# Seven-product first-layer groups: three of four in the last two blocks, with the second layer's first product moved in between

## The chip, the cores and the metric

One core of a Trainium2 chip runs the whole kernel. The metric is the device time of one execution in microseconds (us). The kernel before took 297.75 us (median of three runs, 297.69 to 301.05). Its profiled execution took 297.95 us, of which 296.1 us are the span from the first to the last instruction in the trace.

## The reference

Eight batches, eight heads, 576 positions of head size 64 go through a retention layer (attention without softmax, with a decay per head). Its output, 4608 tokens of 512 channels, goes through a two-layer network with a tanh GELU:

```python
scores = scale * np.matmul(q, k.transpose(0, 1, 3, 2))
ret = scores * Dmat[None, :, :, :]           # Dmat[h, i, j] = gamma_h ** (i - j) for i >= j, else 0
x = np.matmul(ret, v)                        # turned into 4608 x 512
h = x @ w_in                                 # 512 -> 2048
g = 0.5 * h * (1.0 + np.tanh(c * (h + 0.044715 * h * h * h)))
out = g @ w_out                              # 2048 -> 512
```

The change concerns the last two lines alone.

## The kernel before, in words

The kernel is written with the order of every engine's instructions fixed by hand: each engine executes its instructions in the order in which the Python code issues them, and semaphores make it wait where it reads or overwrites what another engine has not finished. TensorE (PE) multiplies into PSUM, of which there are eight banks of 128 x 512 float32 numbers; `bank` takes the bank that has been free longest, `drop` gives one back. ScalarE (ACT) and VectorE (DVE) read PSUM.

The 4608 tokens are taken in nine blocks of 512, `t` = 0 to 8. Blocks 0 to 7 are the first 512 positions of the eight batches; block 8 is made of the last 64 positions of all eight. The retention layer of batch t+1 is worked between the matmuls of block t (the `events`, run at a given step of a block). Blocks 7 and 8 have no retention layer beside them except that of the last tails in block 7.

A block has two layers. Its first layer makes 16 chunks of 128 of the 2048 hidden columns. A plain chunk (`up`) is four matmuls of 512 tokens into one bank `hp` (L471), and one GELU by ACT into the tile `gT` (L477). The second layer is always done by the Strassen-Winograd scheme: tokens and hidden columns are cut in halves, and seven products of half size take the place of eight (`prod`). Each product m has a part for u = 0 and one for u = 1, of eight matmuls of 256 columns each (L661). They land in banks `opA` (products 1 and 2), `opB` (6, 7), `opC` (5, 3) and, in the last two blocks, `opD` (4). The sums of activations that the products need (`act_sums`: s1, s2, an in-place difference in `gT`, s4) are made by DVE, and `after` adds the products up into the two output tiles `o0` and `o1` and stores them.

In the last two blocks (`WIN`) the first layer uses the seven-product scheme too, for two of its four groups. A group j is four chunks: two among the lower eight (`lo`) and two among the upper eight (`hi`). `up_prod(t, j, m)` is product m of group j: four matmuls of 256 columns (L560). Product 1 opens bank `hB`, and ACT copies it to a work tile `s` (L580). Product 2 goes to `hA`, DVE adds it to `s` (L567), and ACT makes the GELU of the sum (L570). Product 6 adds to `hB`, which ACT copies to `v` (L586); product 7 adds to `hB` again, which DVE copies to `u3` and sums with product 5 in `hC` (L588, L589), with a GELU after that; product 4 adds to `hB` and is read by a GELU directly; product 3 adds to `hC`, and `v` plus `hC` gets the last GELU. So one group costs ACT two copies and four GELUs, and DVE one copy and three additions. The sums of weights (`in_sums`) and of the layer's input (`x_sums`) are made by DVE in the second layer of block 6, and of block 7 for block 8's input.

`W_ORDER` is the order of a block's first layer: "mj" is product m of group j, an empty token is the next plain chunk, "aN" is `act_sums` for chunks 2N and 2N+1. After it come the products of the second layer in the order 1, 4, 6, 5, 7, 2, 3.

At the end of block 8, `end` stores each half of an output tile as two stores of 64 rows, one issued by SyncE's queue (SP) and one by ACT's: twelve stores in all. The last product, 3, is read out in two halves: DVE adds the half of u = 0 (L713 in the code calls `add`, whose line is L675) before the half of u = 1 is multiplied into the same bank `opC`.

Of the kernel before, what the change touches and what calls it, by code (L numbers as in the profile page):

```python
# [20 lines left out]
def kernel(  # L21
# [476 lines left out]
        )  # L498
        drop(hp)

    WIN = {t: 2 for t in (NTB - 2, NTB - 1)}
    GW = max(WIN.values())
    wi = {}

    def in_sums(j, ns):
        if not wi:
            for n in "234":
                wi[n] = sb.tile([128, 2, 256 * GW], F16, tag="ld", name="wi" + n, bufs=LD)
        c, lo, hi = slice(256 * j, 256 * j + 256), slice(256 * j, 256 * j + 256), slice(DF // 2 + 256 * j, DF // 2 + 256 * j + 256)
        b11, b12, b21, b22 = w_in_sb[:, 0:2, lo], w_in_sb[:, 0:2, hi], w_in_sb[:, 2:4, lo], w_in_sb[:, 2:4, hi]  # L510
        t2, t3, t4 = (wi[n][:, :, c] for n in "234")
        for n in ns:
            o, x, y, f = {
                3: (t3, b22, b12, ALU.subtract), 2: (t2, t3, b11, ALU.add),
                4: (t4, b21, t2, ALU.subtract), 1: (b12, b12, b11, ALU.subtract),
            }[n]
            nc.vector.tensor_tensor(out=o, in0=x, in1=y, op=f)
# [3 lines left out]
    def x_sums(t):  # L521
        if not xw:
            for n in ("12", "34"):
                x = sb.tile([128, 2, 4, 2, TL], F16, tag="ld", name="x" + n, bufs=LD)
                xw[int(n[0])], xw[int(n[1])] = x[:, 0], x[:, 1]
            for n in range(2):
                for s in "svu":
                    wk[s, n] = sb.tile([128, 512], F32, tag="ld", name="w" + s, bufs=LD)
        o = 8 * (t % 2) if t < B else GM
        x = xT[:, o : o + 8]  # L530
        a11, a12, a21, a22 = x[:, 0:4, 0:2], x[:, 0:4, 2:4], x[:, 4:8, 0:2], x[:, 4:8, 2:4]
        for s, x, y, f in (
            (xw[1], a21, a22, ALU.add), (xw[2], xw[1], a11, ALU.subtract),
            (xw[3], a11, a21, ALU.subtract), (xw[4], a12, xw[2], ALU.subtract),
        ):
            nc.vector.tensor_tensor(out=s, in0=x, in1=y, op=f)

    wk, wb = {}, {}

    def up_prod(t, j, m):  # L540
        if t not in gT:
            gT[t] = sb.tile([128, NF, NI, 128], F16, tag="gT", name="gT", bufs=1)
        o = 8 * (t % 2) if t < B else GM
        lo, hi = 256 * j, DF // 2 + 256 * j
        xh = lambda u, k: lambda kt: xT[:, o + 4 * u : o + 4 * u + 4, 2 * k + kt, :]
        xs = lambda n: lambda kt: xw[n][:, :, kt, :]
        ws = lambda k, c: lambda kt, i: w_in_sb[:, 2 * k + kt, c + 128 * i : c + 128 * i + 128]
        wt_ = lambda n: lambda kt, i: wi[n][:, kt, lo + 128 * i : lo + 128 * i + 128]
        tag, x, w = {
            1: ("B", xh(0, 0), ws(0, lo)), 2: ("A", xh(0, 1), ws(1, lo)), 3: ("C", xs(4), ws(1, hi)),  # L550
            4: ("B", xh(1, 1), wt_("4")), 5: ("C", xs(1), ws(0, hi)), 6: ("B", xs(2), wt_("2")),
# [6 lines left out]
        for i in range(2):  # L558
            for kt in range(2):
# [1 line left out]
                    pb[:, 256 * i : 256 * i + 256].rearrange("p (g t) -> p g t", t=TL), w(kt, i), x(kt),  # L561
                    start=(new and i == kt == 0), stop=(kt == 1), skip_group_check=True,
                )
        s, v, u3 = (wk[n, j % 2] for n in "svu")

        def add(o, a, b):
            nc.vector.tensor_tensor(out=o, in0=a, in1=b, op=ALU.add)  # L567

        def gelu(x, u, f):
            nc.scalar.activation(  # L570
                out=gT[t][:, f : f + 2, 2 * u : 2 * u + 2, :].rearrange("p f i n -> p f (i n)"),
                in_=x.rearrange("p (f n) -> p f n", f=2), func=AF.Gelu_apprx_tanh,
            )

        def free(tag):
            drop(wb.pop((j, tag)))
# [2 lines left out]
        if m == 1:  # L579
            nc.scalar.copy(out=s, in_=pb)  # L580
        elif m == 2:
            add(s, s, pb)
            free("A")
            gelu(s, 0, f)
        elif m == 6:
            nc.scalar.copy(out=v, in_=pb)  # L586
        elif m == 7:
            nc.vector.tensor_copy(out=u3, in_=pb)  # L588
            add(u3, u3, wb[j, "C"])  # L589
            gelu(u3, 1, NH + f)  # L590
        elif m == 4:
            gelu(pb, 1, f)
            free("B")
        elif m == 3:
            add(v, v, pb)
            free("C")
            gelu(v, 0, NH + f)
# [35 lines left out]

    gs = {}

    def act_sums(t, f0, f1, us=slice(0, 2)):
        if t not in gs:
            gs[t] = {n: sb.tile([128, NH, 2, 128], F16, tag="s" + n, name="s" + n, bufs=1) for n in ("1", "2", "4")}
        g = gT[t].rearrange("p f (u i) n -> p f u i n", i=2)
        lo, hi = slice(f0, f1), slice(NH + f0, NH + f1)  # L640
        a11, a12, a21, a22 = g[:, lo, us, 0], g[:, hi, us, 0], g[:, lo, us, 1], g[:, hi, us, 1]
        s = {n: x[:, lo, us] for n, x in gs[t].items()}
        nc.vector.tensor_tensor(out=s["1"], in0=a21, in1=a22, op=ALU.add)  # L643
        nc.vector.tensor_tensor(out=s["2"], in0=s["1"], in1=a11, op=ALU.subtract)
        nc.vector.tensor_tensor(out=a21, in0=a11, in1=a21, op=ALU.subtract)
        nc.vector.tensor_tensor(out=s["4"], in0=a12, in1=s["2"], op=ALU.subtract)  # L646

    def prod(t, m, u):
        g = gT[t].rearrange("p f (u i) n -> p f u i n", i=2)
# [4 lines left out]
        }[m]  # L654
        rhs = {1: W11, 2: W21, 3: W22, 4: wt["4"], 5: wt["1"], 6: wt["2"], 7: wt["3"]}[m]
        tag = {1: "A", 2: "A", 3: "C", 4: "D" if t in WIN else "B", 5: "C", 6: "B", 7: "B"}[m]
        new = m in (1, 6, 5) or tag == "D"
        if new and u == 0:
            op[tag] = bank("op" + tag)
        for f in range(NH):  # L660
            nc.tensor.matmul(  # L661
                op[tag][:, HD * u : HD * u + HD], lhs(f), rhs[:, f],
                start=(new and u == 0 and f == 0), stop=(f == NH - 1), skip_group_check=True,
            )

    keep = {}

    def after(t, m, u):
        last = t == NTB - 1
        if u == 0 and not (last and m == 3) or m == 4 and t in WIN:  # L670
            return
        def pr(tag):
            return op[tag].rearrange("p (u d) -> p u d", u=2)
# [9 lines left out]
                end(o[:, v], i, v)  # L683
        def end(o, i, v, d=slice(0, DM)):
            b = 4 * v + 2 * i
            for h, e in enumerate((nc.sync, nc.scalar)):
                r0 = S * (b + h) + M0
                e.dma_start(out=out[r0 : r0 + TL, d], in_=o[TL * h : TL * h + TL, d])
        if m == 1:
            keep["s1"] = sb.tile([128, 2, HD], F32, tag="k1", name="k1", bufs=1)  # L690
            nc.scalar.copy(out=keep["s1"], in_=pr("A"))
        elif m == 6:
            keep["u2"] = sb.tile([128, 2, HD], F32, tag="k2", name="k2", bufs=1)
            add(keep["u2"], keep["s1"], pr("B"))
        elif m == 7:
            keep["u3"] = sb.tile([128, 2, HD], F32, tag="k3", name="k3", bufs=1)
            add(keep["u3"], keep["s1"], pr("B"))
            keep["o1"] = ost()
            add(keep["o1"][:, :, HD:DM], keep["u3"], pr("C"))
            if t in WIN:  # L700
                drop(op.pop("B"))
                add(keep["o1"][:, :, 0:HD], keep["u3"], pr("D"))
                drop(op.pop("D"))
                send(keep["o1"], 1)
        elif m == 2:
            keep["o0"] = ost()
            nc.scalar.copy(out=keep["o0"][:, :, 0:HD], in_=pr("A"))  # L707
            drop(op.pop("A"))
            if last:
                for v in range(2):  # L710
                    end(keep["o0"][:, v], 0, v, slice(0, HD))
        elif m == 3 and last:
            add(keep["o0"][:, u, HD:DM], keep["u2"][:, u], pr("C")[:, u])  # L713
            end(keep["o0"][:, u], 0, u, slice(HD, DM))
        elif m == 3:
            add(keep["o0"][:, :, HD:DM], keep["u2"], pr("C"))
            drop(op.pop("C"))
            send(keep["o0"], 0)
        elif m == 4:
            add(keep["o1"][:, :, 0:HD], keep["s1"], pr("B"))  # L720
            drop(op.pop("B"))
            send(keep["o1"], 1)
# [88 lines left out]
        for f in events.pop((t, u, last), ()):  # L811
            f()

    W_ORDER = "01 02 p 05 06 p 11 07 p 12 15 04 p 16 03 p 17 a2 p p 14 13 a0 p a1 a3".replace("p", "").split(" ")
    for n in range(2):
        at(NTB - 3, 17 + 2 * n, lambda n=n: in_sums(n, (3, 2)))
        at(NTB - 3, 21 + 2 * n, lambda n=n: in_sums(n, (4, 1)))
    at(NTB - 3, 27, lambda: x_sums(NTB - 2))
    at(NTB - 2, 17, lambda: x_sums(NTB - 1))

# [132 lines left out]
    for t in range(NTB):  # L953
# [7 lines left out]
        else:  # L961
# [7 lines left out]
            todo = deque(f + h for f in range(2 * WIN.get(t, 0), NH) for h in (0, NH))  # L969
            for w in (W_ORDER if t in WIN else ()):  # L970
                def mixed(w=w):
                    if not w:
                        up(t, todo.popleft())
                    elif w[0] == "a":
                        act_sums(t, 2 * int(w[1]), 2 * int(w[1]) + 2)
                    else:
                        up_prod(t, int(w[0]), int(w[1]))
                steps.append((mixed, 0 if w[:1] == "a" else 1 if w else 2))
            for f in range(0 if t == 1 or t in WIN else NH):
                steps.append(lambda f=f: up(t, f))  # L980
                def hi(f=f):
# [1 line left out]
                    if f % 2:  # L983
                        return lambda: act_sums(t, f - 1, f + 1)
                steps.append(hi)
            for m in (1, 4, 6, 5, 7, 2, 3) if t in WIN else (1, 6, 5, 7, 2, 4, 3):
                for u in range(2):
                    steps.append(lambda m=m, u=u: (prod(t, m, u), after(t, m, u)))
        size = sum(s[1] for s in steps if type(s) is tuple)
        u = done = 0  # L990
        for s in steps:
# [41 lines left out]
```

## Time and profile before

| what | us |
|---|---|
| median of the runs | 297.75 |
| profiled execution | 297.95 |
| its span | 296.1 |
| PE busy | 283.0 (96%) |
| DVE busy | 183.5 (62%) |
| ACT busy | 165.9 (56%) |
| block 6, second layer | 224.4 to 238.3 |
| block 7, first layer | 238.3 to 252.5 |
| block 7, second layer | 252.5 to 264.7 |
| block 8, first layer | 264.7 to 277.8 |
| block 8, second layer | 277.8 to 290.9 |
| after the last matmul | 290.9 to 296.1 |

Times in the trace are microseconds from the start of the span. In a timeline a row gives the start, the length, the engine, the source line, the operation and what it writes and reads, then how many instructions it stands for; the square bracket says how long the engine stood idle before it and what ended that. Names ending in q (SPq, ACTq) are the queues that issue transfers. A matmul's modelled length (273 ns for 256 columns) includes the way through the array; the next one starts sooner.

### The profile page before, as it was taken

What the parts mean: (1) busy time and instruction counts of PE and PEld (TensorE: products, weight loads), DVE (VectorE), ACT (ScalarE), POOL (GpSimd) and SP (SyncE); (2) the same over time, 40 slices, a digit from 0 to 9 for tenths busy, and PEclk for the clock granted to TensorE, in tenths of its full rate; (3) what the DMA queues carried; (4) which work ended last, traced back from release to release, by engine and by line L of the source; (5) the groups of instructions that cost most, each with busy time, mean ns of one, the idle gap of its engine ahead of it and who ended that gap; (6) DMA issues with size and microseconds to landing.
All of it is one profiled execution on the core that took longest, in us unless ns stands there. A gap on an engine that the chain in (4) does not pass through costs nothing.

```text
span 296.1 us, 7458 instructions
## 1 busy us (share of the span) xinstructions
PE 283.0 (96%) x3076; PEld 202.0 (68%) x3076; DVE 183.5 (62%) x382; ACT 165.9 (56%) x309; POOL 99.9 (34%) x133
## 2 busy tenths in 40 slices
PE   6779999999999999999999999999999999999992
PEld 2458745888874588458845884488548876886781
DVE  6791506789754874477448744765487867934851
ACT  5377443998239653865386737663765357317600
POOL 4687486960880092008600730067030000000000
PEclk9999999999999999999999999999999999999998
DMA  6999999999969998999799869935931030011005
GB/s 198 310 366 366 341 321 292 273 283 214 201 153 225 214 229 181 253 206 192 95 290 218 148 123 263 216 75 102 254 74 38 2 142 0 2 72 73 0 2 142
DMA packets 129057, 52.91 MB, mean 179 GB/s; under 512 B 101632, under 2 KB 120576, under 8 KB 129024
## 3 DMA queue, kind: packets, MB, share of 16 engines
q1 hardware_dynamic: 128544, 51.92, 75.2%
q10 hardware_dynamic: 480, 0.52, 0.6%
q8 instruction: 24, 0.39, 0.6%
q14 instruction: 9, 0.07, 0.1%
HBM read 36.70 MB, written 9.44 MB: 156 GB/s over the span
## 4 chain that ended last, share of the span: by engine, by line
PE 92%; DVE 3%; ACT 1%; DMA 1%; issue 1%; POOL 0%; SPq 0%; POOLq 0%; DVEq 0%
PE hp L471 28%; PE opB L661 13%; PE opC L661 10%; PE opA L661 10%; PE hp L489 9%; PE op L607 4%; PE hB L560 2%; PE xs L450 2%; PE st L374 2%; PE tr L287 2%; PE xs L441 2%; PE opD L661 1%; PE hC L560 1%; PE xs L364 1%; DMA ld<-in_q_dram 1%; PE st L323 1%
## 5 line engine op out<-in xcount | busy, mean ns | idle before, releaser
L471 PE MATMUL hp<-xT,w_in_sb 128*128 128x512 f16 x384 | 86.9, 379 | 0.0
L477 ACT ACTIVATE gT<-hp 128x512 f16<-128x512 f32 x96 | 54.9, 595 | 31.0 <-PE hp L471 30.5
L471 PEld LDWEIGHTS <-w_in_sb 128*128 128x128 f16 x384 | 37.0, 98 | 40.7
L661 PEld LDWEIGHTS <-gT 128*128 128x128 f16 x512 | 49.0, 98 | 6.6 <-issue 0.2
L661 PEld LDWEIGHTS <-s 128*128 128x128 f16 x384 | 37.0, 98 | 5.6 <-issue 0.7
L643 DVE TENSOR_TENSOR s<-gT 128x512 f16<-128x512 f16 x32 | 14.3, 448 | 28.0 <-ACT gT L477 27.0
L941 POOL COPY gate<-s 128x1 f16<-128x1 f16 x5 | 0.9, 188 | 90.7 <-DVE s L646 90.7
L489 PE MATMUL hp<-xT,w_in_sb 128*128 128x256 f16 x256 | 30.2, 273 | 0.8 <-POOL w_in_sb L735 0.8
L661 PE MATMUL opA<-w_out_sb,gT 128*128 128x256 f16 x256 | 30.6, 273 | 0.0
L425 ACT CAST tbd<-ws 64x256 f16<-64x256 f32 x48 | 19.4, 403 | 16.4 <-DVE ws L416 15.8
L489 PEld LDWEIGHTS <-w_in_sb 128*128 128x128 f16 x256 | 24.5, 98 | 4.5 <-POOL w_in_sb L735 1.1
L661 PE MATMUL opB<-wt,gT 128*128 128x256 f16 x224 | 27.0, 273 | 0.0
L707 ACT COPY ost<-opA 128x512 f32<-128x512 f32 x8 | 4.7, 585 | 38.3 <-PE opA L661 21.7
L383 DVE TENSOR_TENSOR ret<-st,cm 128x512 f16<-128x512 f32 x40 | 24.8, 681 | 0.0
L675 DVE TENSOR_TENSOR k<-k,opB 128x512 f32<-128x512 f32 x16 | 11.0, 687 | 17.8 <-PE opB L661 10.4
L266 POOL TENSOR_TENSOR cq<-ld,sc 128x512 f16<-128x512 f32 x20 | 21.7, 1086 | 0.0
L266 POOL TENSOR_TENSOR ck<-ld,sc 128x512 f16<-128x512 f32 x20 | 21.0, 1049 | 0.0
L460 ACT CAST xT<-xs 128x512 f16<-128x512 f32 x36 | 19.3, 592 | 3.0 <-PE xs L364 1.5
L495 ACT ACTIVATE gT<-hp 128x512 f16<-128x512 f32 x32 | 18.5, 602 | 3.4 <-PE hp L489 3.0
L293 ACT COPY tt<-tr 128x1024 f16<-128x1024 f16 (+1 forms) x12 | 11.8, 998 | 11.1 <-PE tr L287 11.1
L675 DVE TENSOR_TENSOR ost<-k,opC 128x512 f32<-128x512 f32 (+1 forms) x17 | 11.1, 656 | 8.8 <-PE opC L661 8.5
L416 DVE TENSOR_TENSOR ws<-vs,gt 128x256 f32<-128x256 f32 x24 | 15.8, 659 | 1.1
(119 smaller groups left out, 415.1 us busy)
## 6 DMA issues: line engine op xcount, KB each, us to landing
ld<-in_q_dram SPq DMA_DIRECT2D x32, 256.0 KB, 5.2
ld<-in_k_dram SPq DMA_DIRECT2D x32, 256.0 KB, 5.4
ld<-in_v_dram SPq DMA_DIRECT2D x32, 256.0 KB, 5.4
out_dram<-ost SPq DMA_DIRECT2D x16, 512.0 KB, 3.3
ld<-in_moe_w_in_dram SPq DMA_DIRECT2D x16, 256.0 KB, 5.7
ld<-in_moe_w_out_dram SPq DMA_DIRECT2D x16, 256.0 KB, 5.3
lt<-in_k_dram SPq DMA_DIRECT2D x8, 128.0 KB, 5.3
lt<-in_q_dram SPq DMA_DIRECT2D x8, 128.0 KB, 4.6
```

Of the source, the lines that this page charges most:

```text
L266: eng.tensor_tensor(out=dst.rearrange("p (h d) -> p h d", d=D), in0=raw.rearrange("p (h d) -> p h d", d=D), in1=sc[:, s0].unsqueeze(2).to_ ...
L383: nc.vector.tensor_tensor(out=r.rearrange("p (n i) -> p n i", i=128), in0=t.rearrange("p (n i) -> p n i", i=128), in1=(cm if b < PAIR else ...
L416: nc.vector.tensor_tensor(out=w, in0=uc, in1=gt, op=ALU.mult)
L425: cp(out=(tbd[b % 2][r, c, :, r] if c < NC - 1 else tbt[b % NT4][r, :, r]), in_=w[r])
L460: nc.scalar.copy(out=xT[:, g0 : g0 + 2], in_=xs.rearrange("p (n g t) -> p g n t", n=HP, g=2))
L471: nc.tensor.matmul(hp.rearrange("p (g t) -> p g t", t=TL), w_in_sb[:, ct, 128 * fc : 128 * fc + 128], xT[:, o : o + TB // TL, ct, :], star ...
L477: nc.scalar.activation(out=gT[t][:, fc].rearrange("p i n -> p (i n)"), in_=hp, func=AF.Gelu_apprx_tanh)
L489: nc.tensor.matmul(hp[:, 256 * x : 256 * x + 256].rearrange("p (g t) -> p g t", t=TL), w_in_sb[:, ct, 128 * (f + x) : 128 * (f + x) + 128] ...
L495: nc.scalar.activation(out=gT[t][:, f : f + 2, 2 * u : 2 * u + 2, :].rearrange("p f i n -> p f (i n)"), in_=hp.rearrange("p (f n) -> p f n ...
L643: nc.vector.tensor_tensor(out=s["1"], in0=a21, in1=a22, op=ALU.add)
L661: nc.tensor.matmul(op[tag][:, HD * u : HD * u + HD], lhs(f), rhs[:, f], start=(new and u == 0 and f == 0), stop=(f == NH - 1), skip_group_ ...
L675: nc.vector.tensor_tensor(out=o, in0=a, in1=b, op=ALU.add)
```

## The change

First layer of blocks 7 and 8: three groups instead of two go as seven products, so 21 products and four plain chunks take the place of 14 products and eight plain chunks. The sums of weights for the third group are added, in a second set of three tiles, and the work tiles `v` and `u` get a third buffer each. `W_ORDER` is new. GELUs of the seven-product groups are put off on ACT by one token (`due`), and so is the release of bank `hB`.

The two parts of the second layer's product 1 ("Q0", "Q1") are issued between the last first-layer products. The order after them is product 4 (u = 1), 2, 6, 5, 7, 4 (u = 0), 3. The sums s4 move out of `act_sums` to behind product 6. Product 3 gets banks of its own: `opE`, and in block 8 `opE` for u = 0 and `opF` for u = 1. The value `u2` is completed with product 5 by one addition more, so `opC` can be dropped after product 7.

`end` makes one store where it made two: the two 64-row pieces of a half go as one transfer, issued by SP for the half v = 0 and by ACT for v = 1, so six stores end block 8.

```diff
-    WIN = {t: 2 for t in (NTB - 2, NTB - 1)}
+    WIN = {t: 3 for t in (NTB - 2, NTB - 1)}
...
-            for n in "234":
-                wi[n] = sb.tile([128, 2, 256 * GW], F16, tag="ld", name="wi" + n, bufs=LD)
+            for g in range(0, GW, 2):
+                for n in "234":
+                    wi[n, g // 2] = sb.tile([128, 2, 512], F16, tag="ld", name="wi" + n, bufs=LD)
...
-            for n in range(2):
-                for s in "svu":
+            for n in range(3):
+                for s in "svu" if n < 2 else "vu":
                     wk[s, n] = sb.tile([128, 512], F32, tag="ld", name="w" + s, bufs=LD)
...
-        s, v, u3 = (wk[n, j % 2] for n in "svu")
+        s, v, u3 = wk["s", j % 2], wk["v", j % 3], wk["u", j % 3]
...
         def gelu(x, u, f):
-            nc.scalar.activation(
-                out=gT[t][:, f : f + 2, 2 * u : 2 * u + 2, :].rearrange("p f i n -> p f (i n)"),
-                in_=x.rearrange("p (f n) -> p f n", f=2), func=AF.Gelu_apprx_tanh,
-            )
+            g = gT[t][:, f : f + 2, 2 * u : 2 * u + 2, :].rearrange("p f i n -> p f (i n)")
+            due.append(lambda: nc.scalar.activation(
+                out=g, in_=x.rearrange("p (f n) -> p f n", f=2), func=AF.Gelu_apprx_tanh
+            ))
...
             gelu(pb, 1, f)
-            free("B")
+            due.append(lambda: free("B"))
...
+        if t in WIN and m == 3:
+            tag = "EF"[u if t == NTB - 1 else 0]
+        new = tag not in op
...
-            for h, e in enumerate((nc.sync, nc.scalar)):
-                r0 = S * (b + h) + M0
-                e.dma_start(out=out[r0 : r0 + TL, d], in_=o[TL * h : TL * h + TL, d])
+            (nc.scalar if v else nc.sync).dma_start(
+                out=out.rearrange("(b s) d -> b s d", s=S)[b : b + 2, M0:S, d],
+                in_=o[:, d],
+            )
...
             add(keep["u2"], keep["s1"], pr("B"))
+            for f in range(0, NH if t in WIN else 0, 2):
+                act_sums(t, f, f + 2, parts=(1,))
...
+        elif m == 5 and t in WIN:
+            add(keep["u2"], keep["u2"], pr("C"))
         elif m == 3 and last:
-            add(keep["o0"][:, u, HD:DM], keep["u2"][:, u], pr("C")[:, u])
+            add(keep["o0"][:, u, HD:DM], keep["u2"][:, u], pr("EF"[u])[:, u])
             end(keep["o0"][:, u], 0, u, slice(HD, DM))
...
+        elif m == 4 and t in WIN:
+            add(keep["o1"][:, :, 0:HD], keep["u3"], pr("D"))
+            drop(op.pop("D"))
+            send(keep["o1"], 1)
...
-    W_ORDER = "01 02 p 05 06 p 11 07 p 12 15 04 p 16 03 p 17 a2 p p 14 13 a0 p a1 a3".replace("p", "").split(" ")
-    for n in range(2):
+    W_ORDER = (
+        "01 02 05 11 06 12 p 15 07 16 21 22 p 04 25 17 03 26 14 p 13 27 p Q0 24 a0 23 a1 Q1 a3 a2"
+    ).replace("p", "").split(" ")
+    for n in range(GW):
         at(NTB - 3, 17 + 2 * n, lambda n=n: in_sums(n, (3, 2)))
-        at(NTB - 3, 21 + 2 * n, lambda n=n: in_sums(n, (4, 1)))
+        at(NTB - 3, 18 + 2 * n, lambda n=n: in_sums(n, (4, 1)))
...
                 def mixed(w=w):
+                    put_off = list(due)
+                    due.clear()
+                    token(w)
+                    for f in put_off:
+                        f()
...
+                    elif w[0] == "Q":
+                        prod(t, 1, int(w[1]))
+                        after(t, 1, int(w[1]))
...
-            for m in (1, 4, 6, 5, 7, 2, 3) if t in WIN else (1, 6, 5, 7, 2, 4, 3):
-                for u in range(2):
-                    steps.append(lambda m=m, u=u: (prod(t, m, u), after(t, m, u)))
+            two = [(m, u) for m in (1, 6, 5, 7, 2, 4, 3) for u in range(2)]
+            if t in WIN:
+                two = [(4, 1), (2, 0), (2, 1), (6, 0), (6, 1), (5, 0), (5, 1), (7, 0), (7, 1), (4, 0), (3, 0), (3, 1)]
+            for m, u in two:
+                steps.append(lambda m=m, u=u: (prod(t, m, u), after(t, m, u)))
```

## The prediction

> **What bounds the kernel now.** I read the page first, for the chain of work that ended last:
>
> ```profile
> PE 92%; DVE 3%; ACT 1%; DMA 1%; issue 1%; POOL 0%; SPq 0%; POOLq 0%; DVEq 0%
> ```
>
> TensorE sets the time, so a change counts where it takes matmul time away, stops PE, or touches what follows the last matmul. Next I asked for the stretches of the last two blocks; each row gives the length, then busy time and instructions of PE, weight loads, DVE, ACT and POOL, the granted clock and the transfers:
>
> ```profile
> 264.70:277.80 13.10, 13.10 (x90) 8.61 (x88) 7.13 (x13) 9.06 (x18) 0.00 (x0) 1.00 0.19 72
> 277.80:290.90 13.10, 12.58 (x113) 10.84 (x111) 7.70 (x18) 2.56 (x5) 0.00 (x0) 1.00 0.07 18
> 290.90:296.10 5.20, 0.00 (x0) 0.00 (x0) 0.42 (x1) 0.07 (x1) 0.00 (x0) 0.73 0.57 161
> ```
>
> PE is never idle in block 8's first layer, and stands for about half a microsecond in its second; the clock is full (1.00) in both. After the last matmul come 5.2 us without any. The chain in order of time (start, length, what) has the prices of matmuls and the one stop:
>
> ```profile
> 265.30 0.44 PE hA L560 x4
> 265.74 0.86 PE hp L471 x4
> ...
> 288.48 0.89 PE opC L661 x8
> 289.39 0.43 DVE ost L675
> 289.86 1.05 PE opC L661 x8
> 290.93 0.42 DVE ost L675
> ```
>
> A seven-product token (L560, four matmuls of 256 columns) takes 0.4365 us on PE (265.30 to 265.74; the mean over neighbouring tokens has the fourth digit), a plain chunk (L471, four of 512) 0.865 us. The last product stops between its halves: eight matmuls issue in 0.87 us, so the second half could start at 288.31 + 0.87 = 289.18 (288.31 is the timeline's start of the first), but starts at 289.86: 0.68 us lost to the DVE addition on the same bank.
>
> Last, the transfers at the end. The line that issues the final stores, then ACT's queue and ACT's copy before it in the timeline:
>
> ```profile
> L688 SPq DMA_DIRECT2D out_dram<-ost x6: 467/552/597, 288.8 to 292.8; - x6
> L688 ACTq DMA_DIRECT2D out_dram<-ost x6: 497/580/856, 288.8 to 293.2; - x6
> ...
> 290.39 0.58 ACT L707 COPY ost<-opA 128x512 f32<-128x512 f32 x1 [9.97 <-DVE ost L675]
> ...
> 291.00 1.38 ACTq L688 DMA_DIRECT2D out_dram<-ost  x2
> 292.48 1.24 ACTq L688 DMA_DIRECT2D out_dram<-ost  x2
> ```
>
> The last addition is over at 290.93 + 0.42 = 291.35, but ACT issues its last store only at 293.2: the copy of opA stood behind two stores in ACT's queue until 290.39, and four issues of 0.5 to 0.85 us follow it. 2.9 us after the start of that last issue the span ends (2.0 us to landing, 0.9 us for what follows).
>
> **The change part by part.**
>
> *Fewer columns.* One more group per block goes as seven products: 7 x 0.4365 = 3.055 us in place of 4 x 0.865 = 3.46 us. Two blocks: 2 x 0.405 = **0.81 us saved**, all of it on PE's path. (Counting whole blocks: 21 products and 4 chunks are 12.63 us, 14 and 8 were 13.03.) The listing of the changed program has 24 matmuls more, as this needs. Product 1 is moved, not added.
>
> That speaks against the Trainium skill, page "TensorE: Matmul & The Clock Gate", section "Back-to-back issue gap", which gives a sustained spacing of about 81 ns for 128 columns and 131 ns for 512 when each matmul has a weight load. A line through the two puts 256 columns at 98 ns, an estimate, and by it 28 matmuls (2.75 us) would cost more than 16 (2.10 us): 1.3 us lost over two blocks instead of 0.81 won. The rows here say 216 and 109 ns, in proportion to the columns, and I go by them.
>
> *The stop at the end goes.* With opE and opF the second half of product 3 waits for no reader: **0.68 us saved**. What is late next? PE's last matmul is followed by the same 0.42 us addition.
>
> *New waits on PE.* These the trace of before can't show, so I laid the instructions of blocks 7 and 8 out in the changed order, on PE, ACT and DVE at once, with this trace's pitches: ACT 0.49 us from PSUM and 0.52 from SBUF (rows below, start to start), DVE 0.61 for a 128x512 sum from PSUM, 0.34 for an f16 sum, 0.11 more if it needs the one before; results pass on 0.04 us after the end. The old order laid out the same way takes 52.4 us from 238.34 to the last matmul; the trace has 52.55.
>
> ```profile
> 271.34 0.58 ACT L477 ACTIVATE gT<-hp 128x512 f16<-128x512 f32 x1
> 271.82 0.62 ACT L570 ACTIVATE gT<-ws 128x512 f16<-128x512 f32 x1
> 272.34 0.58 ACT L570 ACTIVATE gT<-hB 128x512 f16<-128x512 f32 x1
> 272.82 0.59 ACT L477 ACTIVATE gT<-hp 128x512 f16<-128x512 f32 x1
> ```
>
> The main wait is at product 2 of the second layer, which adds to opA and so needs ACT's copy of product 1 to be over. Count from the issue end of token "23". Its result is there at 0.20, DVE adds until 0.89, ACT's GELU of it starts at 0.93, the copy, queued behind that GELU, at 1.45, and PE may go on at 2.08. Meanwhile PE has only "Q1" and product 4 (u = 1), 2 x 0.87 = 1.74 us: 0.34 us short in block 8 (0.14 of it already spent in Q1, which waits for the GELU of token "24"). In block 7 the tails' products lie between, and 0.10 remains. Two waits of 0.06 and 0.14 come in block 8's first layer, where a product of bank hB follows its copy too closely (one such row exists now: PE idle 0.07 before 273.94). Sum 0.1 + 0.34 + 0.2, **0.63 us lost** unrounded. Behind a waiting PE stands all that follows. Ends: nothing lost, if all pitches are a little shorter; 1.6 us, if ACT takes its full 0.6 us for each and hand-overs cost 0.1. I take 0.63, nearest to the laid-out rows, since the same layout came within 0.2 us for the old order.
>
> *Covered work.* Four more f16 sums of weights in block 6 (4 x 0.36 = 1.4 us of DVE) stand before the masks there. The masks end at 231.97 and their matmuls start at 234.26, so 2.3 us cover the 0.8 us by which the masks move. One DVE addition more per block (0.69 us) and the moved s4 sums (4 x 0.34) lie beside products 5 and 7, 3.5 us of PE; without that cover product 3 would wait by the rest. ACT gets 22 instead of 20 instructions in a first layer: 9.06 us for the 18 recorded is 0.503 each, so 11.1 us in 12.6.
>
> *The end.* Copy of opA and its stores move ahead by some 7 us. After the last matmul's end E remain 0.04 + 0.42 us of addition, one issue on ACT at E + 0.5, the landing, and 0.9. ACT's queue is free by then: its store of o1 is issued at E - 0.5 and takes 0.5 to 0.86. The landing of 128 KB took 2.4 us from SP and 2.9 from ACT (medians); I take 2.6. Ends: 2.0 (64 KB) and 3.3 (512 KB stores), since half a megabyte of o1 is under way at the same time. So E + 4.0 instead of E + 5.2: **1.2 us saved** (0.5 to 1.8).
>
> *Sum.* 0.81 + 0.68 - 0.63 + 1.2 = 2.06. Own time of the profiled execution 297.95 - 2.06 = 295.9 us, span 294.0; that execution is 0.2 above the median, so the median goes from 297.75 to **295.7 us**, 0.7% faster, inside the 2% that count here as no measurable change.
>
> **The rivals.**
>
> *ACT becomes the bound (slower).* Place: the first layers of blocks 7 and 8. Three interleaved groups put 18 instructions into ACT's in-order queue, nine of them waiting for DVE; ACT waited 0.75 + 1.23 + 1.05 us for DVE in block 8's first layer, with two groups. If the third brings half as much again and each instruction takes its mean 0.6 us, 22 x 0.6 + 4.5 = 17.7 us stand against 15.7 us (12.63 of first layer, 1.74 of Q0 and Q1, 0.87 of product 4, 0.44 of product 2) until product 2 needs the last GELU: 2.0 us of stop per block. It decides from 1.3 us per block on, where it eats 0.81 + 0.68 + 1.2. At 2.0 it gives 297.75 + 4.0 - 2.7 = 299.0. For it: ACT will be nearly 90% used there. Against: its pitch is 0.48 to 0.52, and groups in flight overlap their waits.
>
> *The end does not shorten.* The last store lands behind o1's half megabyte: with 3.3 us or more, and waits of 1.2, 0.81 + 0.68 - 1.2 + 0.5 = 0.8 is won: 296.9. For it: 3.1 us was the longest landing of 128 KB in the end phase. Against: 768 KB at the 381 GB/s of the trace's busier slices take 2 us.
>
> *Waits vanish and the landing is short.* 0.81 + 0.68 + 1.8 = 3.3: 294.5.
>
> That the change does not do what it says is ruled out for its counts by the listing: product 3's second half has lost its wait for DVE, and six stores are left of twelve.
>
> **How the numbers follow.** The forecast (295.0 to 296.5) gets 0.62, the unshortened end (296.5 to 297.6) 0.17, the vanished waits (294.2 to 295.0) 0.10, the ACT bound (297.6 to 300) 0.09, and 0.02 for anything else. The range 294.5 to 297.4 takes in both ends of each unknown and leaves out most of the ACT bound. Over 2% faster, 291.8, none of the cases reaches: 0.01. Over 2% slower, 303.7, needs over 4 us of stop per block: 0.02. Within: 0.97.
>
> **What would show it.** Right: block 7 starts as before; PE idle of 0.3 to 1 us from there to the last matmul, the largest piece before product 2 and released by ACT's copy; 51.7 us for that stretch; no idle time before opF; last store issued 0.5 us after the last matmul's end; 4 us from there to the end of the span. Wrong: waits of PE for ACT of over 1 us in a first layer, PE waiting for masks in block 6, or a last landing of over 3.3 us.

## The result

The changed kernel takes 311.34 us (median of four runs, 310.7 to 313.02), the kernel before 299.02 us (median of four). The ratio is 1.0415, 95% interval 1.033 to 1.0499: 4% slower, where 0.7% faster was forecast. The profiled execution took 310.7 us, span 309.0.

The stretches of block 8 in the changed kernel, about as those of before (first layer, with Q0 in it in place of its last two tokens; second layer; after the last matmul; length, busy time and instructions of PE, weight loads, DVE, ACT and POOL, granted clock, share of the transfer engines, GB/s):

```profile
264.00:276.90 12.90, 12.90 (x103) 9.86 (x102) 8.21 (x13) 9.96 (x19) 0.00 (x0) 1.00 0.22 83
276.90:289.60 12.70, 12.55 (x114) 10.72 (x111) 9.91 (x23) 2.93 (x6) 0.00 (x0) 1.00 0.07 20
289.60:309.00 19.40, 0.00 (x0) 0.00 (x0) 0.42 (x1) 0.00 (x0) 0.00 (x0) 0.58 0.12 42
```

Up to the last matmul nothing was lost: it ends at 289.6, and before it ended at 290.9. Then come 19.4 us without a matmul, where 5.2 were and 4.0 were forecast. The last steps of the chain, the line that issues the final stores, and SP's waits:

```profile
288.70 0.89 PE opF L666 x8
289.59 0.02 issue
289.61 0.42 DVE ost L680
```

```profile
L691 SPq DMA_DIRECT2D out_dram<-ost x3: 512/539/680, 282.4 to 289.7; - x3
L691 ACTq DMA_DIRECT2D out_dram<-ost x3: 521/526/1382, 282.4 to 290.1; - x3
```

```profile
SPq L1053 <- DMA out_dram<-ost: 17.7, 1, 17.7
```

The issue of the last of the six stores starts at 290.1, 0.5 us after the last matmul's end, just as forecast. What is late is the data: 17.7 us of waiting for transfers. The same view of stretches shows how they move:

```profile
290.00:294.00 4.00, 0.00 (x0) 0.00 (x0) 0.03 (x1) 0.00 (x0) 0.00 (x0) 0.85 0.13 34
294.00:298.00 4.00, 0.00 (x0) 0.00 (x0) 0.00 (x0) 0.00 (x0) 0.00 (x0) 0.50 0.13 51
298.00:302.00 4.00, 0.00 (x0) 0.00 (x0) 0.00 (x0) 0.00 (x0) 0.00 (x0) 0.50 0.13 51
```

The share is 0.13 and stays there. There are 16 transfer engines, so 0.125 is what two of them give when fully busy, at some 25 GB/s each; sixteen engines busy for an eighth of the time would show the same share, and the packets counted below decide between the two. In the kernel before the same bytes had shares of 0.59 to 0.94 and up to 266 GB/s; its first two stretches of 1 us:

```profile
290.00:291.00 1.00, 0.90 (x8) 0.56 (x6) 0.07 (x1) 0.58 (x1) 0.00 (x0) 1.00 0.94 250
291.00:292.00 1.00, 0.00 (x0) 0.00 (x0) 0.36 (x1) 0.00 (x0) 0.00 (x0) 1.00 0.72 266
```

All tail rows together are 1.05 MB, and 1.05 MB at 51 GB/s are 20.6 us. The granted clock of 0.5 stands beside a PE with nothing to do, and pulls the mean clock of the execution from 0.995 to 0.974: a result of the long end, not a cause.

By this reading the merged store is what made two engines of sixteen. Its output side is two pieces of 64 rows, one for each batch, 576 rows apart; a store of before was 64 rows. The Trainium skill has a rule for it, page "DMA: Bandwidth & Descriptors", section "Why a DMA increments its semaphore by 16 and not by 1": a transfer issued by SP or ACT uses the largest number of engines, up to 16, that divides the size of the slowest dimension on both sides. Here these are 128 partitions and 2 pieces, so two; for 64 and 64 it is sixteen. The experiments test it.

### The profile page after: what moved, and what is told of

It reads as the page before. It is cut to its first block, busy times and chain, and to the rows that moved or that the text cites. A ratio compares the mean times of both kernels' runs of the same rounds, so it can differ in the third digit from the quotient of the medians.

```text
span 309.0 us, 7522 instructions
## 1 busy us (share of the span) xinstructions
PE 282.1 (91%) x3100; PEld 204.2 (66%) x3100; DVE 191.6 (62%) x396; ACT 168.2 (54%) x313; POOL 100.0 (32%) x133
## 5 line engine op out<-in xcount | busy, mean ns | idle before, releaser
L471 PE MATMUL hp<-xT,w_in_sb 128*128 128x512 f16 x352 | 79.0, 379 | 0.0
L477 ACT ACTIVATE gT<-hp 128x512 f16<-128x512 f32 x88 | 50.5, 597 | 31.1 <-PE hp L471 30.5
L471 PEld LDWEIGHTS <-w_in_sb 128*128 128x128 f16 x352 | 34.1, 98 | 38.1
L489 PEld LDWEIGHTS <-w_in_sb 128*128 128x128 f16 x256 | 24.5, 98 | 4.4 <-POOL w_in_sb L746 1.1
L495 ACT ACTIVATE gT<-hp 128x512 f16<-128x512 f32 x32 | 18.5, 602 | 3.4 <-PE hp L489 3.0
L666 PE MATMUL opC<-wt,s 128*128 128x256 f16 x128 | 15.5, 273 | 0.0
```

Of the source, the lines that this page charges most:

```text
L471: nc.tensor.matmul(hp.rearrange("p (g t) -> p g t", t=TL), w_in_sb[:, ct, 128 * fc : 128 * fc + 128], xT[:, o : o + TB // TL, ct, :], star ...
L477: nc.scalar.activation(out=gT[t][:, fc].rearrange("p i n -> p (i n)"), in_=hp, func=AF.Gelu_apprx_tanh)
L489: nc.tensor.matmul(hp[:, 256 * x : 256 * x + 256].rearrange("p (g t) -> p g t", t=TL), w_in_sb[:, ct, 128 * (f + x) : 128 * (f + x) + 128] ...
L495: nc.scalar.activation(out=gT[t][:, f : f + 2, 2 * u : 2 * u + 2, :].rearrange("p f i n -> p f (i n)"), in_=hp.rearrange("p (f n) -> p f n ...
L666: nc.tensor.matmul(op[tag][:, HD * u : HD * u + HD], lhs(f), rhs[:, f], start=(new and f == 0), stop=(f == NH - 1), skip_group_check=True,)
```

## The experiments

E stands for the end of the last matmul. The first matmul of block 6's second layer starts between 223.9 and 226.7 in these profiles, from differences far earlier in the kernel, so times are compared as stretches within one profile.

### Twelve stores again

```diff
-            (nc.scalar if v else nc.sync).dma_start(
-                out=out.rearrange("(b s) d -> b s d", s=S)[b : b + 2, M0:S, d],
-                in_=o[:, d],
-            )
+            for h, e in enumerate((nc.sync, nc.scalar)):
+                r0 = S * (b + h) + M0
+                e.dma_start(out=out[r0 : r0 + TL, d], in_=o[TL * h : TL * h + TL, d])
```

> The changed kernel with the twelve final stores of before (64 rows each, half on SP's queue, half on ACT's); all else as changed. Theory (two engines: a merged store moves on 2 of the 16 DMA engines, and this is the whole loss): the last matmul ends at 289.6 as in the changed kernel's trace, the stores move at over 130 GB/s again, the span ends 4 us later at about 293.6, time 295.5 us, ratio to before 0.992. Rival (the new order of the last two blocks costs time that the end hides, or the lower mean clock is a cause and not a result): 298 us or more.

Measured: 297.06 us against 297.93, ratio 0.9974 (0.9958 to 0.9989). Span 295.8, E = 290.73, so the end takes 5.1 us and not 4. Four stretches of 1 us from E on:

```profile
290.70:291.70 1.00, 0.02 (x1) 0.00 (x0) 0.42 (x1) 0.00 (x0) 0.00 (x0) 1.00 0.41 88
291.70:292.70 1.00, 0.00 (x0) 0.00 (x0) 0.00 (x0) 0.00 (x0) 0.00 (x0) 1.00 0.93 305
292.70:293.70 1.00, 0.00 (x0) 0.00 (x0) 0.00 (x0) 0.00 (x0) 0.00 (x0) 1.00 0.90 287
293.70:294.70 1.00, 0.00 (x0) 0.00 (x0) 0.00 (x0) 0.00 (x0) 0.00 (x0) 1.00 0.33 107
```

With the stores split, shares are above 0.9 and rates around 300 GB/s. Undoing this one part removes the whole loss, and the rest of the change is a small gain. The rival falls. But the end is a microsecond longer than I worked out; that is taken up below.

### The merged stores alone

The kernel before with the opposite edit: six merged stores, everything else as it was.

> The kernel before with nothing changed but the six merged stores. Theory (two engines): all 1.05 MB are issued after 288.8 there, at 51 GB/s that is 20.6 us, from about 290.2 to 310.8, and the span ends near 312, time about 314 us, later than the changed kernel's 311 since its first quarter is not issued ahead. Rival (the loss needs the new order): within 2 us of before.

Measured in one run: 317.3 us, span 315.5, E = 292.3.

```profile
294.00:298.00 4.00, 0.00 (x0) 0.00 (x0) 0.00 (x0) 0.00 (x0) 0.00 (x0) 0.61 0.13 50
298.00:302.00 4.00, 0.00 (x0) 0.00 (x0) 0.00 (x0) 0.00 (x0) 0.00 (x0) 0.50 0.13 51
```

The same two engines, for longer, since no store is issued early here. Its last matmul came 1.4 us later than in the profile of before, and the rest of the gap to 314 is the slow start of the transfers (25 GB/s from 292 to 294). The stores alone make the loss, without any of the new order.

### Eight pieces, four pieces

Same bytes, queues and number of stores; the number of pieces on the output's side differs, eight of 16 rows in the first edit and four of 32 in the second (and so the rows land at other places of the output).

```diff
+            n = M0 + 16 * (2 * v + i)
...
-                out=out.rearrange("(b s) d -> b s d", s=S)[b : b + 2, M0:S, d],
+                out=out.rearrange("(b s) d -> b s d", s=S)[:, n : n + 16, d],
```

```diff
+            n = M0 + 32 * i
...
-                out=out.rearrange("(b s) d -> b s d", s=S)[b : b + 2, M0:S, d],
+                out=out.rearrange("(b s) d -> b s d", s=S)[4 * v : 4 * v + 4, n : n + 32, d],
```

> The changed kernel with merged stores of the same size (128 rows, same bytes, same queues), whose outer dimension on the output's side is 8 pieces of 16 rows in place of 2 pieces of 64; the tail rows land at permuted places of the output. Theory (as many engines as the outer dimension has pieces): 8 engines, a DMA share near 0.5 while the stores last, some 200 GB/s, the last 768 KB take 3.8 us, time about 297.5 us. Rival (a merged store as such is slow, or two large stores per queue are): stays near 311 us with a DMA share of 0.13.

> As the run with 8 pieces, with 4 pieces of 32 rows; the tail rows land at permuted places of the output. Theory: 4 engines, DMA share 0.25, some 102 GB/s, the last 768 KB take 7.5 us from about 290.5 on, span 299.4, time about 301 us. Rival: near 311 us.

Measured in one run of each: 300.95 us with eight, 305.32 us with four. First eight pieces, then four:

```profile
293.00:295.00 2.00, 0.00 (x0) 0.00 (x0) 0.00 (x0) 0.00 (x0) 0.00 (x0) 1.00 0.51 135
295.00:297.00 2.00, 0.00 (x0) 0.00 (x0) 0.00 (x0) 0.00 (x0) 0.00 (x0) 0.60 0.52 173
```

```profile
296.00:298.00 2.00, 0.00 (x0) 0.00 (x0) 0.00 (x0) 0.00 (x0) 0.00 (x0) 0.50 0.26 99
298.00:300.00 2.00, 0.00 (x0) 0.00 (x0) 0.00 (x0) 0.00 (x0) 0.00 (x0) 0.50 0.26 91
```

0.13, 0.26, 0.52 for two, four and eight pieces are 2/16, 4/16 and 8/16: the number of pieces is the number of engines. (These are powers of two; no other number of pieces was run.)

The trace's packets say it without the share. Beside those with data there are packets of 4 bytes, and these rows count them as "under 512 B": for the six stores with two pieces, with four and with eight, and for the last eight of the twelve stores.

```profile
DMA packets 781, 1.07 MB, mean 37 GB/s; under 512 B 12, under 2 KB 524, under 8 KB 780
DMA packets 793, 1.07 MB, mean 30 GB/s; under 512 B 24, under 2 KB 536, under 8 KB 792
DMA packets 817, 1.07 MB, mean 30 GB/s; under 512 B 48, under 2 KB 560, under 8 KB 816
DMA packets 640, 0.79 MB, mean 87 GB/s; under 512 B 128, under 2 KB 384, under 8 KB 640
```

That is 2, 4, 8 and 16 for each store. And counted packet by packet, two are under way at once for 88% of the time from 294 to 304 in the changed kernel (three in the rest), four for 80% of 296 to 300 with four pieces, eight for 72% of 293 to 297 with eight. So few engines are fully busy, not all of them a little. A store being merged, or being large, is not what is slow.

The times are 3.5 and 4.3 us above what I gave: 1.7 and 1.4 us of that is the later E of these profiles (291.3 and 291.0, against the 289.6 I had started from), the rest the transfers' slow first microseconds, which I had not counted.

### Merged the other way

One store for 64 rows and both token halves, which makes the slowest dimension 64 on both sides; in the changed kernel and, alone, in the kernel before. The halves of the last product go as stores of 64 rows, as in the runs with twelve.

```diff
+        def both(o, i, d=slice(0, DM)):
+            rows = out.rearrange("(v b s) d -> b s v d", v=2, s=S)
+            for h, e in enumerate((nc.sync, nc.scalar)):
+                e.dma_start(out=rows[2 * i + h, M0:S, :, d], in_=o[TL * h : TL * h + TL, :, d])
...
-            for v in range(2):
-                end(o[:, v], i, v)
+            both(o, i)
...
-            for v in range(2 if last else 0):
-                end(keep["o0"][:, v], 0, v, slice(0, HD))
+            if last:
+                both(keep["o0"], 0, slice(0, HD))
```

> The changed kernel with stores merged in the other direction: where a whole half of an output tile goes out, one store takes 64 rows of both token halves v, so the outer dimension is 64 on both sides; the last product's two halves keep two stores of 64 rows each. Eight stores in place of twelve or six. Two-engine theory: 64 rows spread over all 16 engines, so merging as such costs nothing; each queue issues three stores behind the o1 addition instead of four small ones, the last starts at E + 0.6 (E is the last matmul's end), lands 2.5 later, the span ends at E + 4.0 instead of E + 5.1 with twelve stores; ratio to before 0.993. Rival (few large stores are slow at the end): no better than twelve stores, 0.997 or above.

> The kernel before with the eight stores of the run before the last, nothing else changed. If the queue of issues held its end, the last issue moves from 293.2 to about 291.4 and the span ends some 1.2 us earlier, ratio 0.996. If the landing of the data held it: same as before, 1.000.

Measured: 297.52 against 298.37 us for the changed kernel so edited, ratio 0.9972 (0.9958 to 0.9986): the same as with twelve stores, with the end at E + 5.5 in its profile and not the 4.0 that was expected. And 298.31 us, ratio 1.0005 (0.9984 to 1.0027), for the kernel before: no gain. Merging in this direction costs nothing (the trace has 16 packets of 4 bytes for each of these stores), so the engines again decide; but fewer issues bring nothing either. The small stores' line in the edited kernel of before:

```profile
L691 SPq DMA_DIRECT2D out_dram<-ost x2: 794/866/937, 291.4 to 292.4; - x2
...
DMA to landing us min/median/max: 2.8/3.2/3.6
```

With fewer stores in the queue each of these issues takes longer (0.87 us, against 0.55 to 0.58 for the last four of twelve), and a 64 KB store lands after 3.2 us instead of 2.1. Still the last issue starts 1.1 us earlier, counted from E: at 292.47 with E = 291.33, against 293.15 with E = 290.91. The end stays at E + 5.2 in both. So the queue of issues was not what held the end of the kernel before.

### Leaving out o1

```diff
-            for v in range(2):
+            for v in range(0):
                 end(o[:, v], i, v)
```

> The changed kernel with twelve stores less the four of output tile o1 in block 8, which are left out (a quarter of the tail rows' output stays unwritten: the o1 halves), so 256 KB instead of 768 KB are left to move after the last matmul. If the data still to be moved hold the end: the span ends at E + 3.6 (issue at E + 0.5, landing 2.2, 0.9 more) instead of E + 5.1. If a fixed delay of the last store holds it: E + 4.8 or more.

Measured in one run: 295.45 us, span 293.7, E = 289.99, so the end takes 3.7 us, and a store lands after 2.1:

```profile
DMA to landing us min/median/max: 1.9/2.1/2.3
```

Output tile o1 is half of the tail rows, 512 KB of 1.05 MB. Four issues go with its data, so this run alone can't tell the two apart; but in the kernel before, with the same bytes, an earlier last issue moved nothing. So the data that are left hold the end. Counted from the issue of o1's stores, the span ends 5.6 us later in the changed kernel with twelve stores (290.18 to 295.8), where 768 KB are still to go, and 7.3 us later in the kernel before (288.81 to 296.1), where 1.05 MB are (the last of them ready only at 291.35).

### One bank for the last product

```diff
-            tag = "EF"[u if t == NTB - 1 else 0]
+            tag = "E"
...
-            add(keep["o0"][:, u, HD:DM], keep["u2"][:, u], pr("EF"[u])[:, u])
+            add(keep["o0"][:, u, HD:DM], keep["u2"][:, u], pr("E")[:, u])
```

This run has the twelve stores.

> The changed kernel with twelve stores, and one bank for both halves of the last product 3. The prediction's term of 0.68 us comes back: PE stands between the two halves, released by the DVE addition, and the stretch from the first matmul of block 7 to the last matmul grows from 51.5 to 52.2 us. Rival (the split of banks saves nothing): 51.5 us.

Measured, from the row of PE's waits:

```profile
PE opE L666 <- DVE ost L680: 0.7, 1, 0.7
```

PE's last part starts at 290.52 instead of 289.67 (288.80 + 0.87), and E is 291.55. The wait is there, and the stretch from block 6's second layer to E grows from 65.7 to 66.5 us, by 0.84. Yet the span is 295.6 us (297.3 us, one run), no more than the 295.8 with two banks: o1's stores are issued at 290.17 and 290.18, and the end follows from them. The time was real on PE (0.84 us here, 0.68 forecast) and worth nothing measurable in this end.

### Order of the copy, and two attempts at a better version

First, a1 behind Q1 in `W_ORDER`, on top of the version merged the other way.

> As the run before, and the activation sums a1 stand behind Q1 instead of ahead of it, so that ACT's copy of product 1 is issued ahead of the GELU of product 3's sum. If the wait before product 2 of the second layer (0.29 us in block 8 of the changed kernel's trace) comes from that copy's place in ACT's queue, it goes and the time falls by 0.2 to 0.3 us; if not, the wait stays, released by something else.

```profile
279.59 1.04 PE L666 MATMUL opD<-wt,gT 128*128 128x256 f16 x8
280.46 1.98 PE L666 MATMUL opA<-w_out_sb,gT 128*128 128x256 f16 x16
```

The 0.29 us before product 2 are gone (279.59 + 0.87 = 280.46), so the cause was the copy's place in ACT's queue. From block 6's second layer to E it is worth 0.14 us (65.54 against 65.68), since waits of 0.07 come in elsewhere. The time is 297.49 us, ratio 0.9986 (0.9964 to 1.0007): a gain of this size doesn't show over the spread of the runs.

Second, o1 prepared and stored earlier:

> A version from what the runs showed. The changed kernel with (1) stores over 64 rows and both token halves, so all 16 engines move them, (2) product 4 complete ahead of product 2 and product 2's second part between 7 and 3, so that o1 is summed from s1 + D and s1 + C prepared earlier and its stores are issued at E - 1.2 instead of E - 0.5, with o0's first half behind them, (3) the sums for the third group moved from block 6 into block 7. Matmuls are the same. Expected by the theory that the data left at the end and a few waits are what remains: waits of 0.14 in block 6 and 0.29 before product 2 go, the span ends at E + 4.2 instead of E + 5.1, together 1.3 us below the changed kernel with twelve stores: ratio to before 0.993. Rival (the end is held by a fixed issue-to-landing time): 0.996.

Measured: 297.32 us, ratio 0.998 (0.9964 to 0.9997). PE does what was asked, E comes 65.3 us after the start of block 6's second layer (66.6 before). But all of the tail rows now leave after 288.29, and 288.29 to the span's end at 295.5 are 7.2 us, as in the kernel before. What o1's head start gives, o0's first half takes back.

Third, the same order of products, but product 2 early and twelve stores, beside the changed kernel with twelve stores again:

> The changed kernel with the twelve stores of before, product 4 complete ahead of product 2 (o1 summed from s1 + D and s1 + C), and the third group's sums of weights moved from block 6 into block 7. Waits of PE in block 6 (0.14) and before product 2 (0.29) go: from the first matmul of block 6's second layer to the last matmul 65.3 us instead of 65.7. The end stays as in the changed kernel with twelve stores, E + 5.1, since 768 KB are left to move as there. Together 0.4 us below that kernel.

> The changed kernel with twelve stores once more, on the same chip as the run before it: the reference for its 0.4 us. Ratio to before 0.997 as measured.

Measured: 296.73 us, ratio 0.9953 (0.9932 to 0.9973), and 297.24 us, 0.9965 (0.9941 to 0.9989). In the profiles E comes 65.3 us after the start of block 6's second layer, against 65.7, as forecast, and the end is E + 5.0 in both. The 0.5 us between the medians fit the forecast of 0.4, but the intervals overlap. The new order has the lowest median of the versions that write the whole output, half a per cent below the kernel before.

## Why the prediction was wrong

*The step that failed* is the landing in "The end": "The landing of 128 KB took 2.4 us from SP and 2.9 from ACT (medians); I take 2.6. Ends: 2.0 (64 KB) and 3.3 (512 KB stores)". I took the duration by bytes alone. Those rows belong to stores whose slowest dimension was 64 or 128 on both sides and which ran on all engines; the merged store of the same size has two pieces on one side and runs on two. No row of the profile of before had such a shape, so the upper end of this unknown should have been a transfer on few engines, not the next larger store on sixteen. With it, the end is the bytes over 51 GB/s: 15.4 us for the 768 KB issued at the end, without the rest of the first 256 KB still in the queue. The 2.6 us of landing became some 17: the last issue starts at 290.1, and the wait for the transfers ends at 307.9. A last landing of over 3.3 us was among the prediction's own signs of being wrong. Twelve stores becoming six was read as a saving of issues only.

*A second step of the same part was wrong, and hidden by the first.* "ACT issues its last store only at 293.2: the copy of opA stood behind two stores" is a true reading, but the end of the kernel before was held by data and not by that queue: with four issues fewer it did not move (1.0005), and without o1's data it fell to E + 3.7. With twelve stores the changed kernel has E + 5.1, so the 1.2 us of this term were 0.1. With twelve stores the whole change gives about half of the forecast 2.06 us: E comes 0.92 us earlier, counted from block 6's second layer (66.59 to 65.67), and the end is 0.1 shorter; the medians were 0.87 and 1.18 us below the kernel before. A quarter of the data now leaves 7 us before E; what that alone is worth was not run.

*The matmuls* came as worked out. From the first matmul of block 7 to E: 51.7 us forecast, 238.07 to 289.58 = 51.5 measured (52.55 before). Block 8's first layer takes 12.81 us (264.05 to 277.73, less 0.87 for Q0), 13.13 before. Its waits are those named: 0.07 and 0.12 on bank hB, 0.05 in Q1, and the largest before product 2.

```profile
277.73 1.08 PE L666 MATMUL opA<-w_out_sb,gT 128*128 128x256 f16 x8
278.65 1.04 PE L666 MATMUL opD<-wt,gT 128*128 128x256 f16 x8
279.81 1.91 PE L666 MATMUL opA<-w_out_sb,gT 128*128 128x256 f16 x16
```

Eight matmuls issue in 0.87 us, so 278.65 + 0.87 = 279.52 would have been possible and 279.81 came, as ACT's copy of opA ran until 279.76. All waits of block 8 sum to 0.53 us (0.54 forecast); block 7's 0.10 did not come.

*The stop at the last product* went as said, and a run with one bank brought it back; that it would be worth its 0.68 us in the end was wrong, as the stores of o1 were issued no earlier for it. In fact they are issued 65.1 us after the start of block 6's second layer, 64.5 before. DVE's three sums for o1 follow product 7, and they start 0.6 us later by that count (286.99 - 223.91 = 63.1, against 286.77 - 224.32 = 62.5), since product 2 (1.75 us) now stands ahead of product 7 and only half of product 4 (0.87 us) moved behind it.

*Covered work*: one cover was thin. In block 6 six sums of weights stand on DVE between the masks and the sum of product 7. Product 4 there starts at 234.58, while the matmuls ahead of it had issued by 233.85 + 0.57 = 234.42: 0.16 us of a wait that I had not named. The masks were in time.

*The rivals*: ACT was not the bound. Its waits for DVE in block 8's first layer were 0.49, 0.26, 0.44 and 0.51 us in the part listed from 267.7 on, and its pitch stayed at 0.46 to 0.54. The case that would not shorten the end (296.9) is nearest to the rest of the change (297.06 and 297.24 with twelve stores), for another reason. That a transfer's shape decides on how many engines it runs was in none of the cases: the six stores were counted, not their shape.

## What to carry to other kernels

Before merging transfers, look at the slowest dimension on both sides: here two, four and eight pieces beside 128 partitions ran on two, four and eight engines, and 64 rows on sixteen, so a store of two pieces of 64 rows runs eight times narrower than one of 64 rows. The share of the transfer engines in the profile shows it at once: 2/16, 4/16, 8/16. And when data are what is left at the end, count the bytes that are issued last: without o1's 512 KB the end fell from E + 5.1 to E + 3.7. PE time saved after the last large store is issued was not saved time here.

## What the runs showed of the hardware that was not expected

The time that a queue needs to issue a store has no fixed price. In the changed kernel with twelve stores a 64 KB store took 0.56 to 0.86 us among the first four, with no other store ahead, and 0.55 to 0.56 us among the last four, with 512 KB ahead. It took 0.79 to 0.94 us in the kernel before with eight stores, and 0.56 to 1.40 us at the end of the changed kernel with eight. The last two merged stores of 128 KB took 5.3 and 8.3 us in the kernel before with six, but 0.51 and 0.52 in the changed kernel with six. The amount of data ahead alone does not explain this, and what sets it was not isolated. So a count of issues times a fixed price is no bound for an end in which data are moving.

Two queues did not widen the transfers. SP and ACT each had merged stores in flight, with 151 packets each from 294 to 304, and the share stayed at 0.13 with two or three packets under way at once; had each queue had two engines of its own, twice that could have been busy. So both used the same two.
